# Attention and two MoE layers on one core: the second MoE's input operands made once, in the first MoE's second pass, and loaded

## The chip, the cores and the metric

One Trainium2 chip, one of its cores. The time is device microseconds of one execution of the whole program. Before the change it is 1921.79 us, the median of three runs (1920.48 to 1923.28).

## The reference, cut to what matters

```python
attn = softmax_d(q) @ (softmax_s(k).T @ v)      # 8 batches, 8 heads, 576 x 64
x = attn as [4608, 512]
y = (silu(x @ w_gate) * (x @ w_val)) @ w_out    # first MoE, d_ff 1536
h = y @ w_in2                                   # second MoE, d_ff 2048
g = where(h > 0, h, exp(min(h, 0)) - 1)         # ELU
out = g @ w_out2
```

All of it is float32 (the weights of the layers come as float64 bits). TensorE takes a float32 value here as a high part and a low part (`hi`, a rounded copy made by ScalarE, and `lo`, the rest, a subtraction), and a product is three matmuls: hi*hi, hi*lo, lo*hi.

## The kernel before, in words

The 4608 tokens are nine blocks of 512. Engines are in-order; the order of the program's text is the order on each engine (`manual_schedule`). PE is TensorE, DVE VectorE, ACT ScalarE, POOL GpSimd; nearly all transfers are issued by SyncE (SP), one queue, in order of the text, and each transfer waits for the one eight before it.

**First MoE** (`run_1`). Two passes ("a" and "b"), each over nine blocks, each with six of the twelve 128-wide slices f. One f of one block is three slots: slot 0 the gate projection (12 matmuls of 512 columns, `proj`), slot 1 the value projection (12), slot 2 the down projection of the f before (12, `emit_B`). Gate and value take turns on two PSUM banks, so the gate of the next f can only start when VectorE has read the last one (`silu_gate`, which needs ScalarE's four activations, `silu_act`). Pass b adds the sums of pass a (`load_yp`) and stores the block's y to DRAM (`ys`). Beside it the weights are converted (`conv`: DVE bits, ACT, POOL). Attention runs beside pass a.

**Second MoE** (`run_2`). The tokens are split once more: h = y @ w_in2 is done as a 2x2 block product with seven multiplications (M1 to M7) in place of eight. Its operands are sums of quarters: on the weights' side they are made by `conv_group` (POOL and ACT, stored in DRAM as `sd` or kept), on the tokens' side by `prep` (lines 905 to 922). Units are block 0 alone, then the pairs (1,2), (3,4), (5,6), (7,8), and all of it twice, once for each half of d_ff. A pair's unit is four steps (`step`); a step is the seven products of one group (42 matmuls), the ELU of its four results on ACT and DVE (`elu_act`, `elu_stt`, `elu_max`, `elu_hi`, `elu_lo`), and in the middle the output product D (`emit_D`, 24 matmuls) of the step before for the unit's first block. After the fourth step comes the unit's end (`after`): D of the last step for the first block, the evacuation of its four PSUM banks (`evac`, lines 1022 to 1046), and D of the second block, 72 matmuls there and 24 in the next unit. D of the second block uses the same four banks as D of the first.

For the next unit `x_tiles` takes the tiles, `y_rows` loads the quarters of y, and `prep` makes the seven operands: four subtractions on POOL (lines 910 to 916), seven `hi` on ACT (line 902) and seven `lo` on DVE (line 903), for each of two halves c of the contraction. In `after` the first `prep` stands ahead of the evacuation:

```python
                    X[nxt] = x_tiles(nxt[1])
                    rows.append(y_rows(nxt[1], 1, more_rows(len(nxt[1]))))
                    prep(X[nxt][0], 0, rows[0])
                dd(u[0], k)()()
```

Of the four `lo` of a step's ELU two are on POOL (`elu_lo(c22, d22, nc.gpsimd)`, and that of `rest12`).

Of the kernel before, what the change touches and what calls it, by code (L numbers as in the profile page):

```python
# [12 lines left out]
ALU = mybir.AluOpType  # L13
# [4 lines left out]
def kernel(  # L18
# [75 lines left out]
    for half in (1, 0):  # L94
        for g in range(half * NG2, (half + 1) * NG2):
            for f in (2 * g, 2 * g + 1):
                chunks.append((("i", f), wsrc_cols(w_in2, f), True))
# [18 lines left out]
    sd = {g: dr.tile([128, 7, 2, 256], FP32, name=f"sd{g}") for g in range(NG2, 2 * NG2)}  # L116
# [97 lines left out]
    def conv_group(g, d1, d2):  # L214
        t = w2_pool[0].tile([128, 7, 2, 256], F32R, tag=f"s{g % NG2}", name="s")
# [20 lines left out]
        if g >= NG2:  # L236
            nc.sync.dma_start(out=sd[g], in_=t.bitcast(FP32))
        else:
            SW[g] = t
# [297 lines left out]
    y2 = [dr.tile([128, KD, TB], FP32, name=f"y2{t}") for t in range(NB)]  # L537

# [322 lines left out]
    XORD = ("M1", "M6", "M5", "M7")  # L861
    XSMALL = ("M2", "M3", "M4")
    X = {}

    def y_rows(blks, c, early):
        if len(blks) == 1:
            r = [early.pop(0) for _ in range(2)]
            for n in range(2):
                nc.sync.dma_start(out=r[n], in_=ys[blks[0]][:, c + 2 * n])
            return (r[0][:, 0:256], r[0][:, 256:512], r[1][:, 0:256], r[1][:, 256:512])  # L870
        r = []
        for n in range(2):
            for b in blks:
                t = early.pop(0)
                nc.sync.dma_start(out=t, in_=ys[b][:, c + 2 * n])
                r.append(t)
        return r

    def x_tiles(u):
        blks = u  # L880
        if len(blks) == 1:
            xa = x_p.tile([128, 4, 2, 2, 256], F32R, tag="x", name="xa")
            o = {op: [xa[:, n, c] for c in range(2)] for n, op in enumerate(XORD)}
            tags = []
            for op in XSMALL:
                tag, t = slot4(("raw", "w", "g"), [128, 2, 2, 256], "xs")
                tags.append(tag)
                o[op] = [t[:, c] for c in range(2)]
            return o, tags
        xs2 = [x_p.tile([128, 2, 2, 2, 512], F32R, tag="x", name="xp") for _ in range(2)]  # L890
        o = {op: [xs2[n // 2][:, n % 2, c] for c in range(2)] for n, op in enumerate(XORD)}
        tags = []
        for op in XSMALL:
            o[op] = []
            for c in range(2):
                tag, t = slot4(("raw", "w", "g"), [128, 2, 512], "xs")
                tags.append(tag)
                o[op].append(t)
        return o, tags

    def split_x(dst, src, eng):
        nc.scalar.activation(out=dst[:, 0, :], in_=src, func=ACTF.Copy)
        eng.tensor_tensor(dst[:, 1, :], src, dst[:, 0, :].bitcast(FP32), op=ALU.subtract)  # L903

    def prep(o, c, rows):
        b11, b12, b21, b22 = rows
        n = b11.shape[-1]
        t1 = tmp_p.tile([128, TB], FP32, tag="e", name="t1")[:, 0:n]
        t2 = tmp_p.tile([128, TB], FP32, tag="th", name="t2")[:, 0:n]
# [3 lines left out]
        split_x(o["M2"][c], b21, nc.vector)  # L913
        nc.gpsimd.tensor_tensor(b12, b22, b12, op=ALU.subtract)
        split_x(o["M5"][c], t1, nc.vector)
        nc.gpsimd.tensor_tensor(b21, b21, t2, op=ALU.subtract)
        split_x(o["M6"][c], t2, nc.vector)
        split_x(o["M3"][c], b22, nc.vector)
        split_x(o["M7"][c], b12, nc.vector)
        split_x(o["M4"][c], b21, nc.vector)  # L920

    def y_tiles(n):
        return [cv_p.tile([128, TB], FP32, tag="cd", name="yr", bufs=NCD) for _ in range(n)]
# [25 lines left out]
    def elu_act(h):  # L949
        e = tmp_p.tile([128, TB], FP32, tag="e", name="e")  # L950
        t = tmp_p.tile([128, TB], FP32, tag="th", name="th")
# [31 lines left out]
    def elu_lo(ch, dst, eng):  # L983
        _, t, _ = ch
        n = TB // len(dst)
        for q, (key, at) in enumerate(dst):
            gt = g_tile(key)
            eng.tensor_tensor(  # L988
# [73 lines left out]

    def step(u, gs_, mid, after=None):
        prev = tail.pop() if tail else None
        p0 = p_bank(0)
        product(p0, "M1", u, gs_, True)
        if prev:
            prev.add()
        p1 = p_bank(1)
        product(p1, "M6", u, gs_, True)  # L1070
        if prev:
            prev.act21()
# [4 lines left out]
        if prev:  # L1077
            elu_stt(prev.c21)
        nc.vector.tensor_tensor(s1, s1, p1, op=ALU.add)
        if prev:  # L1080
            elu_max(prev.c21)
            prev.act12()
            elu_hi(prev.c21, prev.d21)
# [37 lines left out]
        for e in ends:  # L1121
            if e:
                e()
# [303 lines left out]
```

## Time and profile before

| | before |
|---|---|
| median of three runs | 1921.79 us |
| the profiled execution's own time | 1919.87 us |
| its span, first to last instruction | 1918.1 us |
| PE busy | 1739.6 us (91%) |
| DVE, ACT, POOL busy | 1180.5, 908.2, 379.1 us |
| mean granted TensorE clock | 0.964 of 2.4 GHz |
| moved by DMA | 223.99 MB |

Busy time is summed over the whole program. In its slices of 48 us PE stands at nine tenths or more from the fourth to the twenty-second (about 140 to 1000 us) and between seven and nine in most of those behind. What the engines do in a stretch, and what each waited for there, is read from the trace.

### The profile page before, as it was taken

The numbers are of one execution on the slowest core, as the hardware profiler recorded it, in microseconds if no ns is written. First come the engines' busy times: TensorE is split into PE (matmuls) and PEld (weight loads), VectorE is DVE, ScalarE is ACT, GpSimd is POOL, SyncE is SP. The second block draws the span as 40 slices with busy tenths as digits, with TensorE's granted clock in tenths as the row PEclk, the third lists the DMA queues.
The fourth block names the chain that finished last, engine by engine and source line by source line (L and its number), as shares of the span: only waits on it lengthen the run. The fifth ranks groups of instructions, "written<-read, shape, count | busy, mean of one in ns | idle before, by whom it ended". The sixth has DMA issues, their size and how long they took to land.

```text
span 1918.1 us, 21883 instructions
## 1 busy us (share of the span) xinstructions
PE 1739.6 (91%) x8264; PEld 1403.5 (73%) x8264; DVE 1180.5 (62%) x1713; ACT 908.2 (47%) x1604; POOL 379.1 (20%) x300
## 2 busy tenths in 40 slices
PE   5899999999999999999997879796978788969798
PEld 4678888887888888888885767575767566757576
DVE  7768777766866666643456556565544765656563
ACT  5544544444654554433445636363534553635352
POOL 3710000000224441100113131313121322131310
PEclk9899999999999999999998989898989898989899
DMA  9473665734656645532411001010352201112111
GB/s 274 114 206 120 174 164 153 187 89 143 220 175 228 233 165 214 214 121 88 154 61 61 7 26 60 29 55 33 110 198 83 83 12 66 60 50 77 55 44 66
DMA packets 132425, 223.99 MB, mean 117 GB/s; under 512 B 44512, under 2 KB 95712, under 8 KB 124000
## 3 DMA queue, kind: packets, MB, share of 16 engines
q1 hardware_dynamic: 132320, 222.60, 35.8%
q8 instruction: 65, 1.06, 0.2%
q14 instruction: 40, 0.33, 0.1%
HBM read 143.92 MB, written 78.65 MB: 116 GB/s over the span
## 4 chain that ended last, share of the span: by engine, by line
PE 64%; DVE 16%; ACT 12%; issue 5%; POOL 2%; DMA 1%; SPq 0%; DVEq 0%; ACTq 0%; POOLq 0%
PE a L771 10%; PE a L772 10%; PE a L775 10%; PE y L752 9%; PE y L754 9%; PE y L753 9%; PE p L944 6%; ACT th L953 3%; ACT e L954 3%; DVE th L965 3%; ACT e L952 3%; ACT g L979 2%; DVE th L959 2%; DVE g L988 2%; DVE xs L903 2%
## 5 line engine op out<-in xcount | busy, mean ns | idle before, releaser
L771 PE MATMUL a<-x,w 128*128 128x512 f32 x856 | 337.7, 395 | 6.7 <-DVE th L809 6.6
L752 PE MATMUL y<-w,g 128*128 128x512 f32 x576 | 239.6, 416 | 112.6 <-ACT g L979 41.2
L772 PE MATMUL a<-x,w 128*128 128x512 f32 x856 | 334.4, 391 | 0.7 <-POOL x L600 0.7
L754 PE MATMUL y<-w,g 128*128 128x512 f32 x576 | 236.0, 410 | 0.0
L753 PE MATMUL y<-w,g 128*128 128x512 f32 x576 | 235.2, 408 | 0.0
L988 POOL TENSOR_TENSOR g<-th,g 128x512 fp32r<-128x512 f32 (+1 forms) x80 | 96.2, 1205 | 680.4 <-ACT g L979 680.4
L775 PE MATMUL a<-x,w 128*128 128x512 f32 x856 | 228.8, 389 | 0.0
L752 PEld LDWEIGHTS y<-w,g 128*128 128x128 f32 x576 | 115.0, 200 | 147.6 <-ACT g L979 50.0
L959 DVE SCALAR_TENSOR_TENSOR th<-e,th 128x512 f32<-128x512 f32 x144 | 99.4, 690 | 180.0 <-ACT e L954 180.0
L944 PE MATMUL p<-xp,s 128*128 128x512 f32 x768 | 188.8, 398 | 22.6 <-DVE u L1134 16.2
L806 DVE SCALAR_TENSOR_TENSOR th<-th,e 128x512 f32<-128x512 f32 x108 | 79.2, 734 | 202.7 <-ACT th L802 202.7
L771 PEld LDWEIGHTS a<-x,w 128*128 128x128 f32 x856 | 161.4, 189 | 47.1 <-issue 12.5
L944 PEld LDWEIGHTS p<-xp,s 128*128 128x128 f32 x768 | 144.7, 191 | 61.5 <-DVE u L1134 23.4
L784 ACT ACTIVATE g<-th 128x512 fp32r<-128x512 f32 x108 | 68.2, 631 | 251.4 <-DVE th L812 251.4
L772 PEld LDWEIGHTS a<-x,w 128*128 128x128 f32 x856 | 161.5, 189 | 33.9 <-POOL x L600 1.1
L775 PEld LDWEIGHTS a<-x,w 128*128 128x128 f32 x856 | 160.7, 188 | 33.5
L204 POOL TENSOR_TENSOR w<-cd,w 128x512 fp32r<-128x512 f32 x52 | 68.2, 1311 | 576.7 <-ACT w L203 556.1
L753 PE MATMUL y<-g,w 128*128 128x512 f32 x432 | 168.7, 391 | 2.5 <-POOL g L790 2.5
L754 PE MATMUL y<-g,w 128*128 128x512 f32 x432 | 169.0, 391 | 1.8 <-POOL w L204 1.8
L752 PE MATMUL y<-g,w 128*128 128x512 f32 x432 | 169.4, 392 | 1.2 <-ACT w L203 1.2
L944 PE MATMUL p<-xs,s 128*128 128x512 f32 (+1 forms) x720 | 160.1, 370 | 6.2 <-DVE u L1089 6.2
L979 ACT ACTIVATE g<-th 128x512 fp32r<-128x512 f32 (+1 forms) x160 | 91.5, 580 | 142.7 <-DVE th L965 128.4
(186 smaller groups left out, 2887.0 us busy)
## 6 DMA issues: line engine op xcount, KB each, us to landing
xs<-x SPq DMA_DIRECT2D x9, 2048.0 KB, 7.0
x<-xs SPq DMA_DIRECT2D x36, 512.0 KB, 7.0
raw<-in_moe_w_out SPq DMA_DIRECT2D x26, 512.0 KB, 4.0
yr<-ys SPq DMA_DIRECT2D x40, 256.0 KB, 5.6
yp<-ev SPq DMA_DIRECT2D x9, 1024.0 KB, 4.6
ev<-yp SPq DMA_DIRECT2D x9, 1024.0 KB, 7.8
ys<-ev SPq DMA_DIRECT2D x9, 1024.0 KB, 4.0
y<-ev SPq DMA_DIRECT2D x9, 1024.0 KB, 4.9
```

Of the source, the lines that this page charges most:

```text
L204: eng.tensor_tensor(w[:, 1, :], df, w[:, 0, :].bitcast(FP32), op=ALU.subtract)
L752: nc.tensor.matmul(out=ps, lhsT=wh, rhs=xh, start=first, stop=False)
L753: nc.tensor.matmul(out=ps, lhsT=wh, rhs=xl, start=False, stop=False)
L754: nc.tensor.matmul(out=ps, lhsT=wl, rhs=xh, start=False, stop=last)
L771: nc.tensor.matmul(out=ps, lhsT=wh, rhs=x[:, c, 0, :], start=(c == 0), stop=False)
L772: nc.tensor.matmul(out=ps, lhsT=wh, rhs=x[:, c, 1, :], start=False, stop=False)
L775: nc.tensor.matmul(out=ps, lhsT=wl, rhs=x[:, c, 0, :], start=False, stop=(c == KD - 1))
L806: nc.vector.scalar_tensor_tensor(out=t, in0=t, scalar=1.0, in1=e, op0=ALU.add, op1=ALU.mult)
L944: nc.tensor.matmul(out=out_, lhsT=w, rhs=x, start=first and (q, c, k) == (0, 0, 0), stop=(c, k) == (1, 2), skip_group_check=True,)
L959: nc.vector.scalar_tensor_tensor(out=t, in0=e, scalar=1.0, in1=t, op0=ALU.add, op1=ALU.mult)
L979: nc.scalar.activation(out=gt[:, 0, at:at + n], in_=t[:, q * n:(q + 1) * n], func=ACTF.Copy)
L988: eng.tensor_tensor(gt[:, 1, at:at + n], t[:, q * n:(q + 1) * n], gt[:, 0, at:at + n].bitcast(FP32), op=ALU.subtract,)
```

## The change

1. The operands on the tokens' side are made once for each pair of blocks, in pass b of the first MoE, and stored in DRAM (`xd`, seven products of a pair, 1 MB each). `prep_open` loads the quarters of y (half c) into what was a tile for weights (`s0`), `prep_step` does one operand in each slot: subtraction on DVE where there is one, `hi` on ACT, and one call later `lo` on DVE and the store. Three staging places (`n % 3`) are used in turn. Blocks 2 to 7 do one half c each (`side_b`); block 8 does both halves of the pair (6,7), two calls in each slot.
2. The second MoE loads them: `x_big` (two products, 2 MB) and `x_small` (512 KB pieces), 7 MB for a unit. The pairs are now (0,1), (2,3), (4,5), (6,7), block 8 alone comes last, and its operands are made on the spot (`x_one`, ACT and DVE). The second half of d_ff runs through the units backwards, so that block 8 needs no second preparation.
3. All eight weight groups are stored to DRAM and loaded (two tiles `s2`, `s3` for conversion); in block 8 `last_b` loads the first unit's operands and weights.
4. POOL has nothing left in the second MoE; the ELU's four `lo` are on DVE, and the elementwise work of a step has another order. Tiles of the converters (`cd`) hold half of the ELU's.

```diff
+    xd = [
+        {op: dr.tile([128, 2, 2, TB], FP32, name=f"xd{t}{op}") for op in range(7)}
+        for t in range(NB // 2)
+    ]
...
-        nc.gpsimd.tensor_tensor(t1, b12, b11, op=ALU.subtract)
-        nc.gpsimd.tensor_tensor(t2, b22, t1, op=ALU.subtract)
-        split_x(o["M1"][c], b11, nc.vector)
...
+    def x_big(u, ops):
+        t = x_p.tile([128, 2, 2, 2, TB], F32R, tag="x", name="xp")
+        for n, op in enumerate(ops):
+            X[u][0][op] = [t[:, n, c] for c in range(2)]
+            nc.sync.dma_start(out=t[:, n].bitcast(FP32), in_=xd[u[0] // 2][PROD[op]])
+
+    X_HEAD, X_MID, X_LAST = ("M1", "M6"), ("M7", "M5", "M2"), ("M3", "M4")
...
+    def prep_step():
+        if not prep:
+            return
+        if prep["lo"]:
+            op, src, d = prep["lo"]
+            m, c = prep["at"]
+            nc.vector.tensor_tensor(d[:, 1, :], src, d[:, 0, :].bitcast(FP32), op=ALU.subtract)
+            nc.sync.dma_start(out=xd[m][PROD[op]][:, c], in_=d.bitcast(FP32))
+            prep["lo"] = None
+        if not prep["ops"]:
+            prep.clear()
+            return
+        op, src, pre = prep["ops"].pop(0)
+        d = prep["out"][:, prep["n"] % 3]
+        prep["n"] += 1
+        pre()
+        nc.scalar.activation(out=d[:, 0, :], in_=src, func=ACTF.Copy)
+        prep["lo"] = (op, src, d)
+
+    def side_b(i, ff, s):
+        m, c = i // 2 - 1, i % 2
+        if i < 2:
+            return
+        if i < NB - 1:
+            if (ff, s) == (1, 0):
+                prep_open(m, c)
+            elif ff >= 2:
+                prep_step()
+        else:
+            if (ff, s) in ((1, 0), (3, 1)):
+                prep_open(m, ff // 3)
+            elif ff >= 2:
+                prep_step()
+                prep_step()
...
         if (ff, s) == (1, 2):
-            X[0, units[0]] = x_tiles(units[0])
-            last_rows.append(y_rows(units[0], 0, y_tiles(2)))
-            last_rows.append(y_rows(units[0], 1, y_tiles(2)))
-        if ff in (2, 3) and s == 1:
-            prep(X[0, units[0]][0], ff - 2, last_rows[ff - 2])
+            X[units[0]] = ({}, [])
+            x_big(units[0], X_HEAD)
+            x_small(units[0], X_MID, ("raw", "w"))
+            load_s(0)
+            load_s(1)
...
+        if (ff, s) == (HALF - 1, 2):
+            assert not prep
+            x_big(units[0], X_LAST)
+            load_s(2)
+            load_s(3)
...
-        runs = [(half, u) for half in range(2) for u in units]
+        runs = [(0, u) for u in units] + [(1, u) for u in units[::-1]]
...
-                    X[nxt] = x_tiles(nxt[1])
-                    rows.append(y_rows(nxt[1], 1, more_rows(len(nxt[1]))))
-                    prep(X[nxt][0], 0, rows[0])
-                dd(u[0], k)()()
+                    if nxt not in X:
+                        if len(nxt) == 1:
+                            x_one(nxt)
+                        else:
+                            X[nxt] = ({}, [])
+                            x_big(nxt, X_HEAD)
+                            x_small(nxt, X_MID, ("raw", "w", "g"))
+                    if len(nxt) == 2:
+                        x_big(nxt, X_LAST)
+                if len(u) == 1:
+                    rest()
+                dd(u[0], k, drop_w=turn)()
                 if len(u) == 2:
+                    rest()
```

What stands where now, at the three places that the prediction speaks of.

DVE at the end of a pair's unit, before: the last results of the ELU (`g`), then seven `lo` of the next unit's operands (L903), then the evacuation (L1030) on which D of the second block waits.

```order
L988 TENSOR_TENSOR g_9017<-th,g_9017 128x512
L959 SCALAR_TENSOR_TENSOR th<-e,th 128x512
L965 TENSOR_TENSOR th<-th,u 128x512
L903 TENSOR_TENSOR xp<-yr,xp 128x512
L903 TENSOR_TENSOR xs<-yr,xs 128x512
L903 TENSOR_TENSOR xp<-t_9040,xp 128x512
L903 TENSOR_TENSOR xp<-t_9041,xp 128x512
L903 TENSOR_TENSOR xs<-yr,xs 128x512
L903 TENSOR_TENSOR xp<-yr,xp 128x512
L903 TENSOR_TENSOR xs<-yr,xs 128x512
L1030 COPY ev<-y_8696 128x512
```

The same place now: the evacuation (L1087) stands right behind the step's last `lo` (L1045), and what follows it is the fourth result's ELU.

```order
L1016 SCALAR_TENSOR_TENSOR th<-e,th 128x512
L1022 TENSOR_TENSOR th<-th,u 128x512
L1045 TENSOR_TENSOR g_8803<-th,g_8803 128x512
L1087 COPY ev<-y_8499 128x512
L1087 COPY ev<-y_8501 128x512
L1016 SCALAR_TENSOR_TENSOR th<-e,th 128x512
L1022 TENSOR_TENSOR th<-th,u 128x512
L1045 TENSOR_TENSOR g_8861<-th,g_8861 128x512
```

The seven operations between the ELU and the evacuation are gone there (at the one place where block 8 comes next, 22 of 256 columns stand there instead).

SP in block 8 of pass b, now: the loads of y's rows for the preparation (L935), then everything that `last_b` asks for in its first call (xp, xs, s, w), and behind it the first store of an operand (`xd_199`).

```order
L935 DMA yr<-ys_167 128x512
L882 DMA xp<-xd_178 128x2048
L882 DMA xp<-xd_182 128x2048
L872 DMA xs<-xd_183 128x1024 x2
L872 DMA xs<-xd_181 128x1024 x2
L872 DMA xs<-xd_179 128x1024 x2
L1222 DMA s<-sd_100 128x3584
L1222 DMA s<-sd_101 128x3584
L982 DMA w_8062<-wd_108 128x1024
L982 DMA w_8064<-wd_109 128x1024
L982 DMA w_8066<-wd_110 128x1024
L950 DMA xd_199<-xst 128x1024
```

Thirteen loads of 10 MB in all are issued between the two; before, the only loads there were four rows of y and eight of 512 KB of weights, with no store behind them until the block's end.

ACT in the same block, now, from the value of f = 2 to the value of f = 3: `hi` of the operands (L959, `xst`), the `hi` of the first MoE's g (L783) and the four activations of the next gate (L798 to L801).

```order
L959 ACTIVATE xst<-yr 128x512 x2
L783 ACTIVATE g<-th 128x512
L959 ACTIVATE xst<-yr 128x512 x4
L798 ACTIVATE e<-a 128x512
L799 ACTIVATE th<-a 128x512
L800 ACTIVATE e<-e 128x512
L801 ACTIVATE th<-th 128x512
L959 ACTIVATE xst<-yr 128x512
L783 ACTIVATE g<-th 128x512
```

Of the four `xst` in a row the second is the fourth of its half; it takes the first staging place again, which the store `xd_199` has to have left.

## Rows read from the trace of the kernel before

**Rows 1.** Busy time of stretches: block 2 of pass b, block 8, one pair's unit
```profile
core 0: us, PE busy (x) PEld busy (x) DVE busy (x) ACT busy (x) POOL busy (x), PEclk, DMA share, GB/s
650.00:700.00 50.00, 50.00 (x223) 41.40 (x222) 33.55 (x48) 25.27 (x46) 22.58 (x21) 1.00 0.47 163
...
925.70:974.60 48.90, 48.90 (x218) 40.50 (x218) 26.16 (x43) 21.06 (x44) 6.08 (x8) 1.00 0.40 151
...
1136.70:1239.80 103.10, 88.15 (x361) 70.00 (x360) 58.67 (x78) 50.26 (x86) 23.68 (x16) 0.92 0.12 41
```

**Rows 2.** Waits of PE in the second MoE: us in total, times, longest
```profile
PE y L752 <- ACT g L979: 41.2, 12, 7.2
PE y L752 <- DVE ev L1030: 38.2, 4, 12.0
PE y L752 <- DVE ev L1040: 32.9, 3, 12.0
```

**Rows 3.** Timeline of PE (start us, us, [idle before <-releaser]): a step's start, the next's
```profile
1151.67 5.60 PE L944 MATMUL p<-xp,s 128*128 128x512 f32 x24
...
1166.63 1.52 PE L944 MATMUL p<-xp,s 128*128 128x512 f32 x6
```

**Rows 4.** Timeline of PE at the end of the unit (3,4), to the next
```profile
1206.11 0.80 PE L752 MATMUL y<-w,g 128*128 128x512 f32 x1 [3.20 <-ACT g L979]
...
1210.97 0.63 PE L754 MATMUL y<-w,g 128*128 128x512 f32 x1
...
1221.44 0.79 PE L752 MATMUL y<-w,g 128*128 128x512 f32 x1 [9.85 <-DVE ev L1030]
...
1239.82 2.43 PE L944 MATMUL p<-xp,s 128*128 128x512 f32 x10
```

**Rows 5.** Timeline of DVE: operands of block 0 alone, and of a pair
```profile
958.89 0.42 DVE L903 TENSOR_TENSOR xa<-yr,xa 128x256 fp32r<-128x256 f32 x1 [1.00 <-ACT xa L902]
...
1107.03 1.74 DVE L903 TENSOR_TENSOR xs<-yr,xs 128x512 fp32r<-128x512 f32 x1
...
1117.06 1.27 DVE L1030 COPY ev<-y 128x512 f32<-128x512 f32 x2
```

**Rows 6.** Groups by form, second MoE: busy us, mean ns of one
```profile
L988 POOL TENSOR_TENSOR g<-th,g 128x512 fp32r<-128x512 f32 x64 | 84.0, 1313 | 587.5 <-ACT g L979 587.5
...
L988 DVE TENSOR_TENSOR g<-th,g 128x512 fp32r<-128x512 f32 x64 | 44.1, 690 | 30.1 <-ACT g L979 30.1
...
L903 DVE TENSOR_TENSOR xs<-yr,xs 128x512 fp32r<-128x512 f32 x24 | 42.1, 1753 | 0.0
```

**Rows 7.** Timeline of PE in the unit of block 0 alone
```profile
1453.13 4.48 PE L944 MATMUL p<-xs,s 128*128 128x256 f32 x36
...
1461.23 5.99 PE L944 MATMUL p<-xa,s 128*128 128x256 f32 x36 [2.19 <-DVE u L1134]
```

**Rows 8.** Timeline of PE: first and last matmuls of the second MoE
```profile
974.47 1.72 PE L944 MATMUL p<-xa,s 128*128 128x256 f32 x13
...
1913.77 0.39 PE L754 MATMUL y<-w,g 128*128 128x512 f32 x1
```

**Rows 9.** Timeline of ACT in block 8: first activation after the gate of f = 4
```profile
961.13 0.60 ACT L799 ACTIVATE e<-a 128x512 f32<-128x512 f32 x1
```

**Rows 10.** Busy time of a stretch in block 8, DMA in the last two columns
```profile
941.00:955.00 14.00, 14.00 (x64) 11.59 (x63) 7.38 (x12) 7.67 (x17) 4.47 (x6) 1.00 1.02 407
```

**Rows 11.** Timeline of SP's issues in block 8
```profile
935.21 0.32 SPq L847 DMA_DIRECT2D ys<-ev  x1
...
938.60 9.19 SPq L929 DMA_DIRECT2D w<-wd  x8
...
947.84 0.42 SPq L854 DMA_DIRECT2D ev<-yp  x1
```

**Rows 12.** DMA issues: yp in 947 to 949 us, ys on the page (us to landing)
```profile
ev<-yp SPq DMA_DIRECT2D x1, 1024.0 KB, 8.3
...
ys<-ev SPq DMA_DIRECT2D x9, 1024.0 KB, 4.0
```

More of the change, by code (lines that the diff above doesn't have):

```diff
@@ L93 @@
     n_phase1 = len(chunks)
[L94 to L97, printed above, removed]
+    for f in range(F2):
+        chunks.append((("i", f), wsrc_cols(w_in2, f), True))
     for f in range(F2):
@@ L114, in drop @@
         used[tag] -= 1
-    sd = {g: dr.tile([128, 7, 2, 256], FP32, name=f"sd{g}") for g in range(NG2, 2 * NG2)}
+    sd = [dr.tile([128, 7, 2, 256], FP32, name=f"sd{g}") for g in range(2 * NG2)]
     wd = [dr.tile([128, 2, 512], FP32, name=f"wd{f}") for f in range(F2)]
@@ L214, in conv_group @@
     def conv_group(g, d1, d2):
-        t = w2_pool[0].tile([128, 7, 2, 256], F32R, tag=f"s{g % NG2}", name="s")
+        t = w2_pool[0].tile([128, 7, 2, 256], F32R, tag=f"s{2 + g % 2}", name="s")
         st = cv_p.tile([128, 4, 256], FP32, tag="st", name="st", bufs=1)
@@ L879, in x_tiles, with x_small @@
[L879 to L886, printed above, removed]
+    def x_small(u, ops, order):
+        o, tags = X[u]
+        w = TB if len(u) == 2 else TB // 2
+        for op in ops:
+            if w == TB:
+                o[op] = []
+                for c in range(2):
+                    tag, t = slot4(order, [128, 2, TB], "xs")
+                    tags.append(tag)
+                    o[op].append(t)
+                    nc.sync.dma_start(out=t.bitcast(FP32), in_=xd[u[0] // 2][PROD[op]][:, c])
+            else:
+                tag, t = slot4(order, [128, 2, 2, w], "xs")
@@ new lines, in prep_open @@
+    def prep_open(m, c):
+        r = w2_pool[0].tile([128, 7, 2, 256], FP32, tag="s0", name="yr")
+        r = r.rearrange("p a b n -> p a (b n)")
+        for n in range(2):
+            for e in range(2):
+                nc.sync.dma_start(out=r[:, 2 * n + e], in_=ys[2 * m + e][:, c + 2 * n])
+        s_ = w2_pool[0].tile([128, 7, 2, 256], F32R, tag="s1", name="xst")
+        s_ = s_.rearrange("p a b n -> p (a b n)")[:, 0:6 * TB]
+        s_ = s_.rearrange("p (k h n) -> p k h n", k=3, h=2)
+        prep.update(
+            at=(m, c), ops=prep_ops(*(r[:, n] for n in range(6))), out=s_, n=0, lo=None
+        )
@@ L1149 @@
-    units = [(0,)] + [(n, n + 1) for n in range(1, NB, 2)]
+        if prev:
+            k11 = elu_act(p0, False)
+            elu_hi(k12, e12)
+            elu_lo(k12, e12)
+        w = cg()
+        add(w, s1, p2)
+        add(s1, s1, p3)
+        for m in mid:
+            m()
+        if not prev:
+            k11 = elu_act(p0, False)
+        k21 = elu_act(s1, True)
+        elu_stt(k11)
+        elu_max(k11)
+        elu_hi(k11, d11)
+        k22 = elu_act(u3, False)
+        elu_stt(k21)
@@ new lines, in step, with rest, load_s @@
+        elu_max(k21)
+        elu_lo(k11, d11)
+        elu_hi(k21, d21)
+        elu_lo(k21, d21)
+        elu_stt(k22)
+        elu_max(k22)
+        elu_hi(k22, d22)
+        elu_lo(k22, d22)
+        def rest():
+            k12 = elu_act(w, True)
+            elu_stt(k12)
+            elu_max(k12)
+            elu_hi(k12, d12)
+            elu_lo(k12, d12)
+        rot()
+        after(rest)
+    def load_s(g):
+        t = w2_pool[0].tile([128, 7, 2, 256], F32R, tag=f"s{(g + 2) % NG2}", name="s")
+        nc.sync.dma_start(out=t.bitcast(FP32), in_=sd[g])
+        SW[g] = t
@@ L1151, in last_b @@
+    units = [(n, n + 1) for n in range(0, NB - 1, 2)] + [(NB - 1,)]
     def last_b(ff, s):
@@ L1332, in run_2 @@
     def run_2():
-        runs = [(half, u) for half in range(2) for u in units]
+        runs = [(0, u) for u in units] + [(1, u) for u in units[::-1]]
         carry = [flush_b]
         for n, (half, u) in enumerate(runs):
-            nxt = runs[n + 1] if n + 1 < len(runs) else None
-            turn = nxt is not None and nxt[0] != half
+            nxt = runs[n + 1][1] if n + 1 < len(runs) else None
+            turn = nxt == u
             gs = [half * NG2 + g for g in range(NG2)]
```

250 lines of the change are left out of this document (111 added, 139 removed).

## The prediction

> **What bounds the kernel now.** I read the page's slices first: PE is full through the first MoE and gapped in the second, so the second is where time can be had, and the first is where added work can cost. The stretches [rows 1] give the size of a gap: the unit of the pair (3,4) lasts 103.10 us with PE busy for 88.15. The step's timeline [rows 3] gives what it would be without gaps. From one step's first product to the next's it is 1166.63 - 1151.67 = 14.96 us for 66 matmuls (42 products, 24 of D), 0.2267 each. A pair's unit has 4 x 42 + 8 x 24 = 360, so 81.6 us; 21.5 are lost in each.
>
> The waits [rows 2] name the losses: PE on the ELU's last `hi` (41.2 us in 12 waits) and on the evacuation's copy or addition (38.2 + 32.9 in 7). The end of a unit [rows 4] shows both: 3.20 us before D's last part, 9.85 before D of the second block, and behind each the matmuls start 0.43 us apart, the lower level of 1.2 GHz in place of 2.4 (0.92 of full speed granted over the unit [rows 1]). Why the evacuation is late stands on DVE [rows 5]: its copy at 1117.06 comes behind `lo` subtractions of the next operands, of which one takes 1.74 us. Such a subtraction averages 1753 ns beside POOL, where one of the same size by itself takes 690 [rows 6].
>
> For the whole second MoE: first matmul at 974.47, last at 1913.77 [rows 8], some 939.7 us with the end of the last. Its work is eight pairs x 81.6 = 652.9; block 8's (now block 0's) unit twice, 96 x 0.2267 + 168 x 0.124 (36 matmuls of 256 columns in 4.48 us [rows 7]) = 42.6 each, 85.2; and 12 matmuls left over from the first MoE, 2.7. Together 741. So 199 us are waits and slow clock.
>
> **The change, part by part.**
>
> *Preparation out of the units' ends.* 14 `lo`, 14 `hi` and 8 subtractions leave each transition between units, and POOL falls idle. The evacuation then stands behind the ELU alone. By the rows' durations (activations 0.6, DVE 0.69) the ELU of the last step ends thus: M4 is done 9.5 us after the step's start, two DVE additions, three activations, two DVE operations, a `hi` and a `lo` follow, 6 to 8 us; D of the step before covers 5.4 and D's first half, on a result that is ready sooner, 2.7 more. I take no wait there. The evacuation's first copy is 0.69, I take 1 us for it, between nothing (if the ELU ends early) and the present 3.2 and 2.4 (twelve matmuls at 0.43 in place of 0.23 [rows 4]). Seven such ends: 7 us.
>
> *One end keeps its preparation*: block 8 comes after (6,7), and `x_one`'s 22 subtractions of 256 columns, at 0.42 [rows 5] and a little for ScalarE between them 10 us, stand ahead of the evacuation. With the slow matmuls behind it 12.4 us.
>
> *ELU wholly on DVE.* 17 operations x 0.69 = 11.7 us in a step of 14.96; ACT 17 x 0.63 = 10.7. Both fit, with a chain of alternating waits. I give 4 us for all steps, 3 for the first step, where the first MoE's last additions stand on DVE, and 6 for block 8's two units, whose steps are short (2.19 us of such a wait stand there now [rows 7]).
>
> *Loads.* A unit's 7 MB (7340 KB) at the rate that block 8 shows, 407 GB/s [rows 10], take 18 us and about 2 to land. The first tile is free after M6 of the last step; from there to the next unit's M1 PE has 30 products and 120 matmuls of D, 34 us. Covered, and if that cover went, 22 us each with the slow matmuls. At the turn between the halves four weight groups and eight slices of w_out2, 11.5 MB or 28 us, are loaded during block 8's two units of 42.6; the four groups that are new in DRAM cost 7 MB of stores where DMA is at 0.47 [rows 1]. Nothing for either. So the second MoE is 741 + 7 + 12.4 + 13 = 773 us, a gain of 166.
>
> *Work added to the first MoE.* Four pairs x 2 halves x (7 `lo` + 4 subtractions) = 88 on DVE, 61 us, and 56 `hi`, 35 us. In blocks 2 to 7 that is 7.6 us each on a DVE that is busy 33.55 of 50 us where weights are converted and 26.16 of 48.90 in block 8, which has an added preparation of its own to lose [rows 1]. I take nothing for it; where POOL converts, a subtraction may take 1.75 instead of 0.69, 8 us more at worst, if none of it were covered.
>
> *Block 8* is another matter. `last_b` asks for 13 loads, 10 MB, before the first operand's store on SP, and the fourth `hi` on ACT needs that store gone (three staging places). y of block 7 is stored at 935.21 [rows 11] and lands 4.0 later [rows 12]; until then SP waits with the rows of y that need it. Then 768 + 10240 KB = 11.3 MB at 407 GB/s take 27.7 us, the store 1.3 and some 1.6 to land: 969.8. That transfers go in the order of issue is borne out by the sums of block 8's row: the 1 MB issued at 947.84, behind eight of 512 KB, needs 8.3 us to land, against 4.0 with nothing ahead [rows 11, 12]. The Trainium skill says the same against this change (DMA: Bandwidth & Descriptors, Queues, rings and completion order): SP owns one row of rings on the sixteen engines, whose descriptors are consumed in ring order. By that rule the store waits for all 11 MB, as I have it; if the eight in flight shared the engines, it would land about 5 us sooner (issued at 954, eight times its own 0.5 MB to move).
>
> Meanwhile ACT stands at the fourth `hi`, with the gate activations of f = 3 behind it. PE goes on until it wants the bank of that gate again, for f = 4, which now runs 2.7 us before 961.13 [rows 9], so from 958.4. After the landing ACT has nine activations and DVE six operations to do on the path, partly beside each other, about 8.2 us: 978. PE loses 20 us, 2.4 more at the lower clock; the second half's rows of y are then late behind 4.7 MB by the same way, 4 us. Sum 27 with rounding up, between 0 (the stores are not held up) and 35 (as DVE also falls behind).
>
> **Sum.** Against the profiled execution's own 1919.87 us (span 1918.1): - 166 + 27 gives 1781. The median of the runs lies 1.9 above the profiled one, so 1782.
>
> **The rivals.**
>
> *Block 8 is not held up* (stores pass the loads, or the loads are spread): 1782 - 27 = 1755. For it: the lanes let eight transfers run at once. Against it: the landing times above.
>
> *The ELU's chain replaces the preparation*: the wait at the end of a unit stays at 3.2 us with the slow matmuls after it, 5.6 in place of 1 at eight ends, 37 more, 1819. For it: 41.2 us of the waits are on a `hi`, not on the preparation, and POOL's two `lo` of 1.31 us come to DVE [rows 2, 6]. Against it: the new order puts the first block's two results first.
>
> *Operands come too late, slower than before.* Loads wait for tiles; if the first of a unit started only after the transition's last D, not after M6, 20 us and 2.4 of slow clock would show at seven units: 157, hence 1939. It decides from 34 us of delay on. Against it: by the order the tiles' last readers are the products of the last step or D before it.
>
> *It does not do what it says*: the seven operands of a pair are needed in both halves, and each is stored once, loaded twice; the order shows no `lo` of a pair's operands left behind the first MoE. I leave nothing to it.
>
> **How the numbers follow.** Forecast 0.60, at 1782 (its own range 1766 to 1798); block 8 free 0.20; the ELU's chain 0.14; operands late 0.03; others 0.03, mostly between. The range takes in the second case with 7 us below it, since its waits may be nil too, and most of the third: 1748 to 1815. A measurement of this kernel can tell about 0.2%, 4 us, from no change. Faster 0.96, within 0.01, slower 0.03.
>
> **What would show it.** In the trace after: the second MoE from its first product to its last matmul about 773 us, a pair's unit 82 to 84; waits of D on the evacuation near 1 us except once, some 10, at the end of (6,7); no 1.7 us subtractions. In block 8 of pass b a wait of PE of about 20 us with ACT waiting for a DMA store, and a later start of the second MoE, at about 1001. Wrong would be: PE waiting on loads (`xp`, `xs`) at units' starts, D waits of 3 us at each end, or a first MoE that ends where it did.

## The result, and the profile after

The changed kernel takes 1828.01 us (median of 4 runs, 1826.78 to 1831.95) against 1921.14 (4 runs) for the kernel before beside it: a ratio of 0.9517, 95% interval 0.95 to 0.9533. It is faster, as forecast, but by 93 us and not by 140, and the time lies above the range of 1748 to 1815. The profiled execution took 1828.21 us.

The page's head after: PE is busy for 94% in place of 91%, POOL for 9%, and DMA moves 317 MB where it moved 224.

```profile
PE 1713.7 (94%) x8264; PEld 1399.4 (77%) x8264; DVE 1147.1 (63%) x1763; ACT 873.2 (48%) x1534; POOL 164.3 (9%) x140
...
PEclk9899999999999999999998799999989989999999
DMA  9374576543554786777557833314014713341511
...
DMA packets 148360, 317.32 MB, mean 174 GB/s; under 512 B 46240, under 2 KB 97440, under 8 KB 134944
```

Busy time of stretches after, which answers to [rows 1] and has its columns: blocks 1 to 4 of pass b, block 6, block 8 (each from the addition of one block's y to the next one's), and the second MoE from its first product to its last matmul.

```profile
591.80:640.83 49.03, 49.03 (x218) 40.58 (x217) 32.22 (x47) 25.23 (x45) 23.07 (x21) 1.00 0.73 263
640.83:703.87 63.04, 52.30 (x217) 42.12 (x216) 40.55 (x59) 29.10 (x52) 22.14 (x21) 0.92 0.77 279
703.87:765.51 61.64, 51.55 (x216) 41.50 (x215) 39.99 (x58) 28.90 (x52) 15.90 (x13) 0.94 0.76 282
765.51:817.20 51.69, 49.26 (x217) 40.46 (x217) 37.61 (x58) 26.80 (x49) 8.29 (x6) 1.00 0.82 295
868.35:917.31 48.96, 48.96 (x217) 40.54 (x217) 25.70 (x40) 20.95 (x38) 1.30 (x1) 1.00 0.54 194
966.27:1048.79 82.52, 55.49 (x219) 44.45 (x219) 32.81 (x52) 23.98 (x43) 0.00 (x0) 0.81 0.88 334
1041.10:1822.10 781.00, 752.77 (x3421) 624.61 (x3419) 452.03 (x710) 381.82 (x661) 0.00 (x0) 0.98 0.33 127
```

The second MoE takes 781.0 us in place of 939.7 [rows 8]: 158.7 won. Its first product stands at 1041.10 instead of 974.47: 66.6 of that are given back in pass b. Blocks 2 to 5 give back 32.2: by the same cut they took 48.99, 48.45, 48.96 and 48.96 before, and take 63.04, 61.64, 51.69 and 51.15 now. Blocks 6 and 7 give back nothing, block 8 up to the first product 33.1, and 1.4 stood ahead of block 2 already.

The waits of PE after, over the whole program, beside [rows 2]:

```profile
PE a L770 <- DVE th L808: 57.4, 11, 20.8
PE y L751 <- ACT g L1036: 11.5, 2, 5.8
PE y L751 <- DVE ev L1087: 9.3, 1, 9.3
...
PE p L997 <- DVE u L1121: 6.6, 4, 2.6
```

The three waits of the second MoE that made 112 us before are 20.8 now, and a new one leads the list: the gate's product (L770) waits for the bank that DVE's multiplication with the gate (L808) reads. What it waits for in turn shows on ACT and SP. First block 8 (ACT, then SP's issues):

```profile
984.97 0.62 ACT L959 ACTIVATE xst<-yr 128x512 fp32r<-128x512 f32 x1
1005.07 0.63 ACT L959 ACTIVATE xst<-yr 128x512 fp32r<-128x512 f32 x1 [19.48 <-DMA xd<-xst]
```

```profile
968.77 0.32 SPq L846 DMA_DIRECT2D ys<-ev  x1
...
984.73 2.95 SPq L982 DMA_DIRECT2D w<-wd  x3
988.62 20.19 SPq L950 DMA_DIRECT2D xd<-xst  x5
```

The `hi` at 1005.07 has waited 19.48 us for a store of an operand to leave its staging place, and the next gate's activations stand behind it. That store is the first of the three that SP issues between 988 and 992 us. They are behind the loads, and take 16.3 us each from issue to landing (the median of all 14 stores of the block is 5.7):

```profile
xd<-xst SPq DMA_DIRECT2D x3, 512.0 KB, 16.3
```

The same wait for a place stands in block 2, where it was not forecast:

```profile
666.61 0.63 ACT L959 ACTIVATE xst<-yr 128x512 fp32r<-128x512 f32 x1 [0.53 <-DMA xd<-xst]
...
676.36 0.63 ACT L959 ACTIVATE xst<-yr 128x512 fp32r<-128x512 f32 x1 [6.24 <-DMA xd<-xst]
...
681.27 0.63 ACT L959 ACTIVATE xst<-yr 128x512 fp32r<-128x512 f32 x1 [3.72 <-DMA xd<-xst]
```

DVE in block 2 shows two things more: it stands for rows of y that land late, with the gate's work (L805) behind it, and one `lo` takes 2.88 us where others take 0.69, while POOL runs a subtraction of the conversion (second view).

```profile
657.22 0.69 DVE L917 TENSOR_TENSOR yr<-yr 128x512 f32<-128x512 f32 x1 [4.64 <-DMA yr<-ys]
657.83 0.69 DVE L805 SCALAR_TENSOR_TENSOR th<-th,e 128x512 f32<-128x512 f32 x1
...
663.87 2.88 DVE L949 TENSOR_TENSOR xst<-yr,xst 128x512 fp32r<-128x512 f32 x1
```

```profile
663.77 2.42 POOL L231 TENSOR_TENSOR s<-st,s 128x1024 fp32r<-128x1024 f32 x1
```

In the second MoE (timeline of PE) the plain ends of units have no wait at all: pairs' units start at 1122.04, 1204.04 and 1286.04, 82.00 us apart, where 81.6 is the work. The end before block 8 alone waits for the evacuation as before, and block 8's own end (1424.03) for a result:

```profile
1122.04 2.88 PE L997 MATMUL p<-xp,s 128*128 128x512 f32 x12
...
1204.04 2.88 PE L997 MATMUL p<-xp,s 128*128 128x512 f32 x12
...
1361.15 0.80 PE L751 MATMUL y<-w,g 128*128 128x512 f32 x1 [9.27 <-DVE ev L1087]
...
1424.03 0.80 PE L751 MATMUL y<-w,g 128*128 128x512 f32 x1 [5.77 <-ACT g L1036]
```

Open after this: in pass b, whether staging places, the order on SP's queue, the work on DVE or the sheer volume cost the 65 us; in the second MoE, what the 5.77 us at each end of block 8's units are. The runs' medians below stand beside the change's 1828.0; the kernel before gave 1920.8 to 1921.9 beside each of them.

### The profile page after: what moved, and what is told of

Its sections match the earlier page's. It is cut to its first block, busy times and chain, and to the rows that moved or that the text cites. A ratio compares the mean times of both kernels' runs of the same rounds, so it can differ in the third digit from the quotient of the medians.

```text
span 1826.3 us, 21717 instructions
## 1 busy us (share of the span) xinstructions
PE 1713.7 (94%) x8264; PEld 1399.4 (77%) x8264; DVE 1147.1 (63%) x1763; ACT 873.2 (48%) x1534; POOL 164.3 (9%) x140
## 3 DMA queue, kind: packets, MB, share of 16 engines
q8 instruction: 65, 1.06, 0.2%
## 4 chain that ended last, share of the span: by engine, by line
PE 78%; DVE 8%; DMA 7%; ACT 5%; issue 1%; POOL 1%; SPq 1%; DVEq 0%; ACTq 0%; POOLq 0%
PE p L997 17%; PE y L753 11%; PE y L751 11%; PE y L752 10%; PE a L770 9%; PE a L771 9%; PE a L774 9%; DMA xd<-xst 3%; DMA yr<-ys 2%; PE t L431 1%; PE t L590 1%; DVE u L1121 1%; ACT th L1010 1%; ACT e L1011 1%; DVE g L1045 1%
## 5 line engine op out<-in xcount | busy, mean ns | idle before, releaser
L770 PE MATMUL a<-x,w 128*128 128x512 f32 x856 | 343.4, 401 | 57.6 <-DVE th L808 57.4
L771 PE MATMUL a<-x,w 128*128 128x512 f32 x856 | 338.5, 395 | 0.7 <-POOL x L599 0.7
L751 PE MATMUL y<-w,g 128*128 128x512 f32 x576 | 227.7, 395 | 20.8 <-ACT g L1036 11.5
L770 PEld LDWEIGHTS a<-x,w 128*128 128x128 f32 x856 | 163.9, 191 | 103.2 <-DVE th L808 56.8
L774 PE MATMUL a<-x,w 128*128 128x512 f32 x856 | 232.0, 393 | 0.0
L753 PE MATMUL y<-w,g 128*128 128x512 f32 x576 | 227.7, 395 | 0.8
L752 PE MATMUL y<-w,g 128*128 128x512 f32 x576 | 226.8, 394 | 0.0
L1121 DVE TENSOR_TENSOR u<-u,p 128x512 f32<-128x512 f32 x180 | 123.4, 686 | 139.7 <-PE p L997 131.8
L771 PEld LDWEIGHTS a<-x,w 128*128 128x128 f32 x856 | 164.1, 192 | 34.5 <-POOL x L599 1.2
L774 PEld LDWEIGHTS a<-x,w 128*128 128x128 f32 x856 | 163.1, 191 | 34.6
L997 PE MATMUL p<-xp,s 128*128 128x512 f32 x768 | 182.3, 391 | 3.9 <-DVE u L1121 3.9
L783 ACT ACTIVATE g<-th 128x512 fp32r<-128x512 f32 x108 | 68.3, 632 | 241.6 <-DVE th L811 241.6
L805 DVE SCALAR_TENSOR_TENSOR th<-th,e 128x512 f32<-128x512 f32 x108 | 77.5, 717 | 159.7 <-ACT th L801 159.7
L997 PE MATMUL p<-xs,s 128*128 128x512 f32 (+1 forms) x720 | 154.6, 369 | 0.4 <-DVE u L1121 0.4
L751 PEld LDWEIGHTS y<-w,g 128*128 128x128 f32 x576 | 110.0, 191 | 44.8 <-ACT g L1036 12.4
L997 PEld LDWEIGHTS p<-xs,s 128*128 128x128 f32 x720 | 126.4, 189 | 23.4 <-DVE u L1121 0.6
L798 ACT ACTIVATE e<-a 128x512 f32<-128x512 f32 x107 | 63.8, 597 | 168.0 <-PE a L774 167.9
```

The costliest lines, as they stand in the source:

```text
L751: nc.tensor.matmul(out=ps, lhsT=wh, rhs=xh, start=first, stop=False)
L752: nc.tensor.matmul(out=ps, lhsT=wh, rhs=xl, start=False, stop=False)
L753: nc.tensor.matmul(out=ps, lhsT=wl, rhs=xh, start=False, stop=last)
L770: nc.tensor.matmul(out=ps, lhsT=wh, rhs=x[:, c, 0, :], start=(c == 0), stop=False)
L771: nc.tensor.matmul(out=ps, lhsT=wh, rhs=x[:, c, 1, :], start=False, stop=False)
L774: nc.tensor.matmul(out=ps, lhsT=wl, rhs=x[:, c, 0, :], start=False, stop=(c == KD - 1))
```

## The experiments

**Blocks 2 to 7: more staging places.** `lo` is written over its source, so the seven `hi` have a place each.

```diff
+            if m < 3:
+                lo = src.bitcast(F32R)
+                nc.vector.tensor_tensor(lo, src, d.bitcast(FP32), op=ALU.subtract)
+                nc.sync.dma_start(out=xd[m][PROD[op]][:, c, 0], in_=d.bitcast(FP32))
+                nc.sync.dma_start(out=xd[m][PROD[op]][:, c, 1], in_=src)
...
-        d = prep["out"][:, prep["n"] % 3]
+            d = prep["out"][:, prep["n"] % (7 if small else 3)]
```

> Blocks 2 to 7 of pass b store an operand's hi and lo apart: hi in one of seven places, lo over its source. So no hi of these blocks has to wait for a store. The elementwise work is the same (7 hi, 7 lo, 4 subtractions), the bytes too, the stores twice as many; block 8 is untouched. Theory S (ScalarE stands at a hi that waits for a staging place, because the store is late behind other transfers on SP's one queue; waits of 6.2 and 3.7 us in block 2): blocks 2 and 3, now 63.0 and 61.6 us, fall to 49 to 53 (the late rows of y remain, some 2 us), blocks 4 and 5 to 49 to 50: 23 to 31 us less, 1797 to 1805. Rival W (the added work on VectorE, slow beside POOL's conversion, is what holds the gate's bank): the blocks stay at 60 to 63, the time within 4 us of 1828. Rival D (more stores are dearer on SP): slower than 1828.

1809.46 us, 18.5 less, 4 short of theory S. Blocks 4 and 5 are at 48.96, block 2 at 53.3, block 3 at 56.9. So S holds for 19 of the 32 us; 13 are left in blocks 2 and 3. The stores now being twice as many cost nothing that can be seen. What is left shows in block 3 of this run, first on DVE, then on ACT:

```profile
711.45 0.69 DVE L929 TENSOR_TENSOR yr<-yr 128x512 f32<-128x512 f32 x1 [6.02 <-DMA yr<-ys]
...
718.45 2.50 DVE L967 TENSOR_TENSOR yr<-yr,xst 128x512 fp32r<-128x512 f32 x1
```

```profile
738.55 0.63 ACT L201 ACTIVATE w<-cd 128x512 fp32r<-128x512 f32 x1 [5.80 <-DMA wd<-w]
```

Rows of y are late, a `lo` takes 2.50 us beside POOL's 2.41 us subtraction, and ACT waits for the conversion's own place, whose store (`wd`) stands behind operands' stores.

**The same, with the preparation two slots later.**

```diff
-            elif ff >= 2:
+            elif (ff, s) >= (2, 2):
                 prep_step()
```

> As the run with seven places, and in blocks 2 to 7 the eight calls of the preparation start two slots later, so that the rows of y have some 9 us more to land. Theory R (what was left in blocks 2 and 3 with seven places, 4 and 8 us, is VectorE standing for rows that land late, 6.0 us in block 3, with the gate's silu behind it): blocks 2 and 3 at 49 to 51, 1800 to 1805. Rival W (it is the added work beside POOL's conversion, subtractions of 1.7 to 2.5 us): 1807 to 1812. Rival T (the weights' own place, for which ScalarE waits 5.8 us there, behind the operands' stores): the wait late in block 3 stays, 1804 to 1808.

1801.85 us, 7.6 less than with places alone: theory R, though not to its end. Block 2 is at 50.8, block 3 at 53.2, 6 us of the 13 less; 7 are left. No `hi` and no subtraction of these blocks waits for rows of y any more. One wait of 2.69 us stays late in block 3 behind ACT's 4.93 us for `wd`: rival T's remainder. W's forecast of 1807 to 1812 is missed; the added work is all still there, and how much of the 7 us is its share was not tried. Nor do the bytes by themselves cost the time in blocks 2 and 3: the same 35 MB are moved there in this run, at 0.93 and 0.92 of the DMA engines, and the two blocks take 104 us in place of 125.

```profile
641.80:692.62 50.82, 49.81 (x218) 40.36 (x217) 43.86 (x58) 28.91 (x52) 24.16 (x21) 1.00 0.93 338
692.62:745.86 53.24, 50.41 (x215) 40.99 (x214) 40.47 (x58) 28.61 (x52) 16.39 (x13) 0.97 0.92 334
```

**Block 8: stores on another queue.**

```diff
-            nc.sync.dma_start(out=xd[m][PROD[op]][:, c], in_=d.bitcast(FP32))
+            (nc.gpsimd if m == 3 else nc.sync).dma_start(
+                out=xd[m][PROD[op]][:, c], in_=d.bitcast(FP32)
+            )
```

> In block 8 alone the 14 stores of operands are issued by POOL, which has no other work there, instead of SP; everything else is as in the changed kernel. Theory S (the store stands behind 11 MB of loads on SP's queue): PE's wait of 20.8 us in block 8 falls below 8, the one of 6.3 with it, the time by 15 to 25 us, to 1803 to 1813. Rival B (bandwidth: the loads hold the DMA engines, whoever issues the store): the wait stays above 15, the time within 5 us of 1828. Blocks 2 to 7 are the same in both.

1825.17 us, 2.8 less, where the change's own four runs lie 5.2 us apart: outside both forecasts for the wait, and inside B's for the time. PE's waits in block 8:

```profile
1006.53 0.80 PE L770 MATMUL a<-x,w 128*128 128x512 f32 x1 [13.24 <-DVE th L808]
...
1029.44 0.79 PE L770 MATMUL a<-x,w 128*128 128x512 f32 x1 [11.61 <-DVE th L808]
```

20.8 + 6.3 became 13.2 + 11.6. The DMA issues say why (KB each, median us to landing): first the stores of the first half, 983 to 1006 us, then all weights of 966 to 1040.

```profile
xd<-xst POOLq DMA_DIRECT2D x7, 512.0 KB, 10.3
```

```profile
w<-wd SPq DMA_DIRECT2D x8, 512.0 KB, 22.7
```

A store by POOL does not stand behind all of SP's loads: beside them it lands in 10.3 us, where the first three on SP took 16.3. ACT still waits for a place four times in the first half, 13.2 us in all. And the weights, 6.2 us in the change, now take 22.7, and ACT's first `hi` of the second half waits 14.9 for its rows. Part of the wait changed its place. By the Trainium skill (DMA: Bandwidth & Descriptors, Issuing engines are not separate DMA queues) transfers run on the same engines whoever issues them and interleave, and another issuer saves only the time of issuing; the run agrees in the total, 2.8 us of 33.

**Block 8: places.** As the run with the later start, seven places in block 8 too.

```diff
-            if m < 3:
+            if m < 4:
```

> As the run with seven places and the later start, and now block 8 too takes seven places for each of its two halves; its loads and stores, in bytes and in order, are those of the change. In the first half no hi waits for a store; the rows of the second half take the places of the first and wait until these stores have left. Theory P (it is the places: with enough of them the first half's stores may land when they like): the wait of 20.7 us goes, block 8 falls from 82 to 50 to 60 us, 1770 to 1782. Theory V (it is the volume, 24.3 MB in the block: what doesn't wait for a store in the first half waits for rows in the second): the wait moves to the second half, 12 us or more there, block 8 stays over 65 us, 1785 to 1800.

1802.19 us against 1801.85: nothing. That is against theory P, and 2 us above V's range. The first half's wait is gone and PE has one of 30.89 us in the second half, behind the rows of y (ACT, then SP's wait before it issues them):

```profile
1000.13 0.63 ACT L984 ACTIVATE xst<-yr 128x512 fp32r<-128x512 f32 x1 [31.00 <-DMA yr<-ys]
```

```profile
SPq L947 <- DMA xd<-yr: 8.1, 1, 8.1
```

The rows take the places in which the first half's `lo` stand, and SP waits 8.1 us until the last of these has been stored. So the run trades one wait for a place for another, and does not rule places out.

**Block 8: loads behind the stores.**

```diff
-        if (ff, s) == (1, 2):
+        if (ff, s) == (4, 2):
             X[units[0]] = ({}, [])
...
-        if s == 2 and ff >= 1:
+        if s == 2 and ff >= 4:
```

> As the change, but what block 8 asks for ahead of its first operand's store (10 MB: operands, weight groups, weights) is asked for behind its last store, 3 f later. Bytes are the same, only their order is other. If order alone decides: both waits (20.8 and 6.3 us) go, and what is left is the first product of the second MoE waiting for the 2 MB of its operands, 3 MB behind them and its weight group, 6.8 to 8.7 MB at 407 GB/s, 17 to 22 us from an issue some 12 us ahead of it: 5 to 12 us of wait and the slow clock, 1808 to 1817. If the volume decides (24.3 MB that have to move between the start of the block and the first steps of the second MoE): PE waits there for nearly as long as it does now in block 8, 20 us and more for operands and weights together, 1822 to 1832.

1832.09 us, at the upper end of the forecast for the volume; the forecast for order alone fails. In block 8 two waits of 2.2 and 3.3 us are left, and the second MoE begins with these:

```profile
1038.46 5.06 PE L997 MATMUL p<-xp,s 128*128 128x512 f32 x12 [19.43 <-DMA s<-sd]
...
1055.83 4.45 PE L997 MATMUL p<-xp,s 128*128 128x512 f32 x10 [5.48 <-DMA xp<-xd]
```

30.5 us in four waits, where there were 27.0 in two (and 1.4 at the first product's bank). It does not follow that the bytes alone force them. Until the put-off loads were issued, at 1017.56, the DMA engines were far from full, and full only after it:

```profile
969.03:1017.56 48.53, 42.96 (x180) 34.38 (x180) 27.88 (x44) 20.65 (x38) 0.00 (x0) 0.96 0.62 228
1017.56:1060.00 42.44, 17.53 (x59) 13.50 (x58) 12.11 (x18) 6.98 (x12) 0.00 (x0) 0.68 1.01 405
```

An order that spreads the loads over the first stretch was not tried.

**Less to move in block 8.** First 4.7 MB of the loads in block 7:

```diff
+                        if (i, ff, s) == (NB - 2, HALF - 1, 0):
+                            X[units[0]] = ({}, [])
+                            load_s(0)
+                            load_s(1)
+                            x_small(units[0], X_MID[:1], ("raw", "w"))
```

> Two weight groups and two of the six small pieces, 4.7 MB of the 10 MB that block 8 asks for ahead of its first store, are loaded in block 7 instead. Theory S: at 407 GB/s the store lands 11.5 us sooner, PE's wait of 20.8 falls to 8 to 10, the time by 10 to 14 us, to 1814 to 1818. Rival W (two operands in each slot are too much for VectorE and ScalarE in block 8): under 4 us. Rival B (the block is bound by bandwidth as a whole): what is moved out of it comes back at once, 11 us too; against S it would also shorten the wait of 6.3 in the second half.

1818.10 us, 9.9 less, just short of S's range and of B's 11; PE's waits are 9.85 and 7.16, so the second did not shrink, which speaks for S here and not for B. By itself the run does not decide. Then the whole preparation of the pair (6,7) out of block 8, into the second MoE (`late_open` takes free tiles for the rows, `side` is called at three points of a step):

```diff
+    SIDE = [(0, 0, 1), (1, 1, 1), (1, 2, 1)]
...
+                early = half == 0 and u in units[1:3]
+                side_n[0] = SIDE[k] if early else (0, 0, 0)
+                if early and k == 0:
+                    late_open(NB // 2 - 1, units.index(u) - 1)
```

> The pair (6,7) is not prepared in block 8 of pass b but in the second MoE, half c = 0 during the unit (2,3) and half c = 1 during (4,5): the same operations, in steps 0 to 2 of each, with free tiles of the weights as places for the rows and the operands. Theory B (block 8 is bound by what it moves, 24.3 MB in 966 to 1040 us at 328 GB/s; order on a queue alone gave 2.8 us back): without 7.3 MB of stores and 2.1 MB of rows 14.9 MB are left, 304 GB/s over 49 us; both waits (20.8 and 6.3) go, block 8 falls from 82.5 to 50 to 56 us, the units (2,3) and (4,5) stay at 82 to 83: 1795 to 1803. Rival O (orders of 10 MB of loads still fill the block, so the rows of yp and the weights come late instead): a wait of 8 us or more stays in block 8, 1805 to 1815. Rival E (eight operands between the ELU's links make a step's results late): PE waits for g or u in six steps, 2 us and more each, and 1812 to 1825.

1806.33 us, 21.7 less, outside theory B's 1795 to 1803. Block 8 in this run:

```profile
967.32:1016.76 49.44, 49.44 (x219) 40.94 (x219) 18.94 (x29) 16.27 (x29) 0.00 (x0) 1.00 0.95 380
```

49.44 us in place of 82.52, PE full, DMA at 0.95 and 380 GB/s: the block's 33 us are gone as theory B has it, and rival O's wait is not there. Eleven of them came back in the second MoE, 5.5 and 5.8 in the units (2,3) and (4,5): rival E's kind of wait, though in one step of each unit (3.15 and 3.20 us) and not in six, for an addition of `u` behind an operand's `lo` on DVE.

The edit takes three things out of block 8 at once: 9.4 MB, the preparation's instructions and its places. What the bytes alone can cost is estimated from the change's stretch from the block's start to the second MoE's first product, which lasted 41.76 us before:

```profile
966.27:1041.10 74.83, 47.80 (x185) 38.06 (x185) 28.83 (x46) 21.60 (x39) 0.00 (x0) 0.79 0.87 330
```

That is 24.7 MB. At 380 to 407 GB/s (this run, [rows 10]) they take 61 to 65 us, so by this estimate the bytes force at most 19 to 23 of the 33 us. In the rest the DMA engines had less to do, for the order or the places; the runs do not tell these apart.

**The other pairs moved within pass b**, on top of that: none in blocks 2 and 3, (2,3) whole in block 6, (4,5) whole in block 7.

```diff
-        if i < 2:
+        if i < 4 or i == NB - 1:
             return
-        if i < NB - 1:
+        if i < 6:
+            m, c = 0, i - 4
```

> As the run with the pair (6,7) in the second MoE, and the others moved within pass b: none in blocks 2 and 3, the pair (0,1) in blocks 4 and 5, (2,3) whole in block 6, (4,5) whole in block 7, two calls in each slot there. Three staging places as in the change. Theory (the loss of blocks 2 and 3 comes from transfers: conversion's loads and stores, 0.77 of the DMA engines, with stores late behind them; blocks 6 and 7 have 0.50 to 0.54 and a half adds 4.7 MB, 96 GB/s): blocks 2 and 3 at 49, 4 and 5 at 51 to 52, 6 and 7 at 49 to 51: 24 to 28 us less than the run before it, 1769 to 1777 if that gives 1797 to 1801. Rival (three places for two operands in each slot hold ScalarE as in block 8): 5 to 10 us of waits in each of blocks 6 and 7, 1782 to 1795.

1799.28 us: 7 less, not 24 to 28. Blocks 2 and 3 are at 49.0 and 48.4, but block 4 at 54.2, 5 at 51.9, and 6 and 7 at 57.8 and 57.9. The rival's waits are there (6.4 us of PE in block 6), its cause only in part: ACT waits 0.28 us for a place in block 6 and 3.75 in block 7, 4.70 and 3.88 for rows of the second half, and DVE and ACT wait for each other between two operands of one slot (block 6):

```profile
866.45 0.63 ACT L978 ACTIVATE xst<-yr 128x512 fp32r<-128x512 f32 x1 [0.28 <-DMA xd<-xst]
...
877.82 0.64 ACT L978 ACTIVATE xst<-yr 128x512 fp32r<-128x512 f32 x1 [4.70 <-DMA yr<-ys]
...
889.57 0.63 ACT L978 ACTIVATE xst<-yr 128x512 fp32r<-128x512 f32 x1 [2.09 <-DVE yr L917]
```

How the 9 us of each of these blocks divide over these was not tried.

**The end before block 8 alone:** the evacuation ahead of `x_one`.

```diff
                 dd(u[0], k, drop_w=turn)()
+                if nxt and nxt not in X:
+                    x_one(nxt)
```

> At the end of the unit (6,7) the evacuation and then the preparation of block 8's operands, in place of the other order. Theory: the wait of 9.27 us for the evacuation and 2.4 to 3.3 us of slow clock behind it go, and the 10 us of preparation hide beside 72 matmuls (16 us) of the second block: 1815 to 1817. Rival: the preparation, now behind the copies and beside the ELU of the fourth result, is late for the next unit's first product; PE waits there as long, 1826 to 1830.

1818.41 us, 9.6 less, just above the 1815 to 1817 of the theory. The wait of 9.27 is gone and the unit (6,7) takes 81.98 in place of 94.18; block 8's two units give 1.6 back (56.18 and 54.67 for 55.43 and 53.81).

**Block 8's results in other tiles.**

```diff
-            G2[key] = slot4(("g", "w", "raw"), [128, 2, TB], "g2")
+            one = key[0] == NB - 1
+            G2[key] = slot4(("w", "raw", "g") if one else ("g", "w", "raw"), [128, 2, TB], "g2")
```

> In block 8's two units the ELU's results take tiles of the weights first, in place of the three of the tag g; nothing else. Theory: of the 5.8 us that PE waits at each of the two ends, 3.2 are ScalarE's wait for a place that the D before is still reading (its hi at 1416.94 waits 3.17 us for the matmul y); they go, and with them part of the 2.4 us of slow clock: 1819 to 1823. Rival: the chain of the last step's ELU is itself that long, and the place costs nothing: 1826 to 1830.

1815.45 us, 12.6 less, more than the 5 to 9 forecast: the two waits of 5.8 are 0.78 and 2.73, and the slow matmuls behind them go too. Most of the wait was a place that D still read, not the ELU.

**Together:** places, later start, (6,7) in the second MoE with its calls spread otherwise, evacuation first, other tiles.

```diff
-    SIDE = [(0, 0, 1), (1, 1, 1), (1, 2, 1)]
+    SIDE = [(0, 1, 2), (1, 1, 1), (1, 1, 0)]
```

> What the runs have shown to help, together: seven places and the later start in blocks 2 to 7, the pair (6,7) in the second MoE (its calls spread more evenly over the steps than in the first try), the evacuation ahead of block 8's operands, block 8's results in tiles of the weights. By sums from the run with places and later start, 1801.9: less 33 us in block 8, plus 2 to 11 in the units (2,3) and (4,5), less 9.6 and 12.6 at the last two: 1749 to 1758. If the preparation between the ELU's links costs as before, 1755 to 1760; if the parts cover the same microseconds, 1760 to 1770.

1752.06 us (5 runs, 1747.34 to 1754.39), 0.9126 of the kernel before [0.9114, 0.9138]: faster than both kernels, and what the sum of the parts gave. The units (2,3) and (4,5) take 85.6 each, 3.6 over the others where the first spread cost 5.5 and 5.8. The busy line of its page, and its three largest waits of PE from pass b on:

```profile
PE 1693.4 (97%) x8264; PEld 1384.5 (79%) x8264; DVE 1145.9 (66%) x1763; ACT 871.5 (50%) x1534; POOL 166.0 (10%) x140
```

```profile
PE p L1037 <- DVE u L1162: 11.5, 9, 2.6
PE y L751 <- ACT g L1077: 3.5, 2, 2.7
PE a L770 <- DVE th L808: 3.5, 3, 2.3
```

## Why the prediction was wrong

**The step that failed** is one sentence on the work added to the first MoE: "I take nothing for it", of the "7.6 us each on a DVE that is busy 33.55 of 50 us" in blocks 2 to 7. It weighed the work against DVE's free time, and DVE had that time: it is busy for 40.6 of block 2's 63.0. What it left out are the places, and when the transfers land. The text had found the mechanism for block 8 (three staging places, a store late on SP, ACT at the fourth `hi`, the gate's activations behind it), and did not put the same question to blocks 2 and 3, where [rows 1] shows DMA at 0.47 before and where conversion's loads and stores, 2 MB of x and 1 MB of yp share the queue. The runs split the 32.2 us of blocks 2 to 5: places 19, rows of y that land late 6; of the 7 left, the conversion's own store and subtractions beside POOL were not told apart. The "8 us more at worst" had been looked for on DVE beside POOL, where at most those 7 lie; the 8 itself does not come out of its rows (a block's eleven subtractions at 1.06 us more are 11.7).

**Block 8** was forecast at 27 us and took 33.1; PE's wait of 20 was 20.77, ACT did stand at a store, the second half's 4 was 6.26. The mechanism was what the trace shows: from the issue of y's store (968.77) to the `hi` that the operand's store lets go (1005.07) it is 36.3 us, for 34.6 in the sum. It is not the whole cause in the sense that undoing it would help: with the order, the queue or the places changed, each by itself, the time stays within some 4 us. What ended the waits was taking the preparation out, its bytes with its work and places; less to load ahead of the store took 9.9 us. The sum went by the time of 11.3 MB, and so the size came out nearly right. The rule of the Trainium skill that the prediction used (DMA: Bandwidth & Descriptors, Queues, rings and completion order), that the descriptors of SP's rings are consumed in order, agrees with the trace: the first three stores landed behind the loads, 16.3 us after their issue, and those on another queue in 10.3. The rival "block 8 is not held up" at 1755 fell with its condition: the stores do not pass the loads, and none of the three changes tried frees the block.

**The second MoE** was forecast at 773 and took 781.0. Right: no waits at the ends of pairs' units (0.4 us over the work of 81.6, where 1 was given), and 12.2 at the end of (6,7) for 12.4. Mis-sized: block 8's two units, given 6 us of waits in all, took 55.43 and 53.81 for a work of 42.6 each: 24. The text priced the ELU's links and looked at a wait for `u` [rows 7]; the larger part was a tile of `g` that comes free only when D has read it. The rival "ELU's chain" (1819) came nearest to the time, which is luck: its 3.2 us ends appear nowhere at pairs. (Its 1819 counts eight ends where the forecast counts seven; with seven it is 1814.)

**The sum**: -158.7 in place of -166, +66.6 in place of +27, hence 1828 for 1782. Of the 46 us missed, 32 are the "nothing" of blocks 2 to 7, 6 block 8, 7 the second MoE and 1 stood ahead of block 2. The signs announced in block 8 came true; "the second MoE starts at 1001" did not, at 1041.

## What to carry to other kernels

When work is moved beside a full engine, count for each block not only its time on the helping engines but the bytes it adds and the places that must come free for its next instruction: a helper that waits in order for a store holds everything behind it, though it is half idle. If a wait for DMA sits in a stretch at nine tenths of the DMA engines, sum the bytes up to the point where they are needed, and estimate what they alone force. Here three changes of order, queue and places only moved the wait, and taking the transfers out of the stretch, with their work, ended it. A high share by itself proves nothing: blocks 2 and 3 stood at 0.93 and 0.92 with the later start, and lost only 2 and 5 us. A wait for a result at a unit's end may be a wait for the place of that result, and then costs one line to mend.

## What the runs showed of the hardware

Block 8 ran at 380 GB/s over 49.44 us with DMA at 0.95 while PE lost nothing. Blocks 2 and 3 of the run with places and the later start moved 338 and 334 GB/s while PE lost 2 and 5 us. Beside some 10 MB of loads on SP's queue a store of 512 KB took 10.3 us to land from POOL's queue (median of seven), against 16.3 on SP's own behind them (median of three), while the median of SP's weights went from 6.2 to 22.7. A `lo` of 0.69 us took 2.88 (the change, block 2) and 2.50 (seven places, block 3) while POOL ran a subtraction of 2.4 us.
